# Attention steps of block 3 moved between slots, its last stores split between two queues, and its turned chunks placed elsewhere

## The chip, the core and the metric

The kernel runs on one core of one Trainium2 chip. Times are device microseconds of one launch; the profile is one execution taken by the hardware profiler, and its times count from the span's start. The engines are TensorE (PE, and PEld for its weight loads), VectorE (DVE), ScalarE (ACT), GpSimd (POOL) and SyncE (SP). SP computes nothing and issues DMAs; GpSimd and ScalarE issue DMAs too.

## What is computed

A normalized input goes through an attention over eight positions (two apart, looking back) and through a feed-forward layer with a squared ReLU. Both results and the input are added.

```python
def _A_ref(x, wqkv, wo):                 # S = 2048, D = 576, H = 32 heads of 18
    qkv = (x @ wqkv).reshape(B, S, 3, H, Dh)...
    idx = pos[:, None] - arange(8) * 2   # masked where negative
    logits = einsum("bhsd,bhswd->bhsw", q, kg) * Dh ** -0.5
    o = einsum("bhsw,bhswd->bhsd", softmax(logits), vg)
    return o.reshape(B, S, D) @ wo

def _B_ref(x, w1, b1, w2, b2):           # F = 4608
    r = max(x @ w1 + b1, 0)
    return (r * r) @ w2 + b2

xn = layernorm(x)
return x + _A_ref(xn, wqkv, wo) + _B_ref(xn, w1, b1, w2, b2)
```

## The kernel before

**Tiles and stages.** The sequence is cut into four blocks of 512 rows (b = 0 to 3), and the heads into four groups (g = 0 to 3). Matmuls have float32 accuracy from two parts: ScalarE copies a value to a rounded high part, VectorE subtracts that from the value and so makes the low part ("split", `..._hi` and `..._lo`); products are hi x hi, hi x lo and lo x hi. The feed-forward products of two blocks are combined so that fewer matmuls are needed (names T1 to T4, B11 to B22, `S`, `X`). The stages in order: the qkv products of blocks 0 and 1; `phase_a(0)`, feed-forward of both and second product of block 0; `phase_b0`, second product of block 1, then the qkv products of blocks 2 and 3 in four quarters ("quads"); `phase_a(1)`; `phase_b1`, which begins with `phase_blocks` (35 steps, k = 0 to 34, second product of blocks 2 and 3 in combined form) and ends block 3 with 16 "single tiles" (m = 0 to 15) of 14 matmuls each, the products with `wo` in five chunks c = 0 to 4, and `tail`.

**Attention on VectorE.** `attention(b, g)` is a generator of 19 steps: four times a product with the keys (`pr<-q,kv`) and its sum (`lg<-pr`), the maximum, the exponential on ScalarE, the division, then four times a product with the values (`pr<-lg,kv`) and three additions (`pr<-pr` twice, `q<-pr`). After the last additions the result q goes to DRAM in eight stores (`o<-q`), four for each of two parts of the columns. `side(n)` runs n steps where the code calls it, and tables of digits say how many: `QUADS` in the quads, `SPOTS` in `phase_a(1)`, `LAST` at the 35 steps k, `SINGLES` at the 16 tiles m. `complete(b)` runs what is left of a block's attention. The engines run their queues in the order in which the code is written.

**The end of block 3.** At m = `DUE`, or when no attention is left, `regroup(3, 0)` and `regroup(3, 1)` read the two stored parts back (`st<-o`, `r<-o`, issued by GpSimd). `o_hi(b, c)` turns a chunk with a transpose on VectorE (L1040, the last one L1045 with L1055 and L1056) and copies its high part on ScalarE; `o_lo` makes the low part on VectorE. `w2_hi` and `w2_lo` split the weights of the tile two ahead (w2s, three buffers: a split waits until TensorE has left the tile before the current one); `w2_lo` also issues the load of the tile five ahead (w2r, on SP). `h_hi` and `h_lo` split the next pair's operand (h). Chunk 4's weights are split last, at c = 2. In `tail` TensorE multiplies chunks 3 and 4, and drains and stores of the output follow.

Of the kernel before, what the change touches and what calls it, by code (L numbers as in the profile page):

```python
# [20 lines left out]
NB = S // TB  # L21
# [4 lines left out]
G = 4  # L26
# [6 lines left out]
L = P // G  # L33
# [11 lines left out]
ROWS = {(4 * b - 1 + k // 3, k % 3): (b, h) for b in (2, 3) for k, h in ((0, 0), (2, 2), (3, 1), (5, 2), (6, 2))}  # L45
PIECES = (0, 0, 0, 2, 3, 4, 0, 3, 2, 0, 2, 2, 1, 0, 3, 2, 4, 5)
SPOTS = ('000002', '120012', '100024', '010023', '110023', '111022', '110023', '100024', '010024', '120022', '110023', '110023', '120014', '110021', '110024', '110023', '110110', '000100')
QUADS = ('01111111111010', '10100010101110', '00110111111111', '10010000111111', '00000000000001', '00111010101010')
LAST = '00000111010011010011000101000011021'
SINGLES = '2222121212010000'  # L50
DUE = 10
TIMES = (2, 2, 3, 5, 6, 8, 10, 11, 14, 15, 17, 18, 19, 19, 22, 24, 27, 27, 29)
DRAINS = (14, 21, 24, 29, 26)
PAIRED = (*range(1, NP - 2, 2), NP - 2, NP - 1)
# [9 lines left out]
def block_kernel(ctx: ExitStack, tc: tile.TileContext, x, xt, wqkv, wo, w1, b1, w2, b2, w1l, w2q, w2l, w2x, out):  # L64
    nc = tc.nc
# [65 lines left out]
    def tt(out, a, b, op):  # L131
        return nc.vector.tensor_tensor(out=out, in0=a, in1=b, op=op)  # L132
# [18 lines left out]
    def four(dt=F32):  # L151
        return sb.tile([P, 2, TB], dt, name="r4", bufs=4)
# [210 lines left out]
    def shifted(t, j, *dims):  # L363
        a = t[:, j:j + 1, 0:1]
        return bass.AP(tensor=a.tensor, offset=a.offset, ap=[a.ap[0], [DIL * CG, W], *dims])

    loads, landed, queue, free, lane, kept_back = [], {}, [], [0], [nc.sync], [0]
# [17 lines left out]
    def release():  # L385
        free[0] += 1
        fetch()
# [10 lines left out]
    def attention(b, g):  # L398
        k, q = landed.pop(("k", b, g)), landed.pop(("q", b, g))
        lg = sb.tile([P, NA, W], F32, name="lg")  # L400
        mx = sb.tile([P, NA], F32, name="mx")
        sm = sb.tile([P, NA], F32, name="sm")
        for j in range(NJ):
            pr = sb.tile([P, W, CG], F32, name="pr")
            tt(pr, q[:, j:j + 1].to_broadcast([P, W, CG]), shifted(k, j, [1, CG]), ALU.mult)
            if j == NJ - 1:
                release()
            yield
            nc.vector.tensor_reduce(out=lg[:, j * HG:(j + 1) * HG].rearrange("p a w -> p w a"),  # L409
                                    in_=pr.rearrange("p w (a d) -> p w a d", d=DH), axis=AX.X, op=ALU.add)  # L410
            yield
        if b == 0:
            l4 = lg[:4].rearrange("p (j h) w -> p j h w", j=NJ)
            tt(l4, l4, mask[:4, :, None].to_broadcast([4, NJ, HG, W]), ALU.add)
        nc.vector.tensor_reduce(out=mx, in_=lg, axis=AX.X, op=ALU.max)
        tt(lg, lg, mx[:, :, None].to_broadcast([P, NA, W]), ALU.subtract)
        yield "exp"
        nc.scalar.activation(lg, lg, AF.Exp, scale=SCALE)
        yield
        nc.vector.tensor_reduce(out=sm, in_=lg, axis=AX.X, op=ALU.add)  # L420
        nc.vector.reciprocal(sm, sm)
        tt(lg, lg, sm[:, :, None].to_broadcast([P, NA, W]), ALU.mult)
        yield
        v = landed.pop(("v", b, g))
        for j in range(NJ):
            pr = sb.tile([P, W, CG], F32, name="pr")
            at = lg[:, j * HG:(j + 1) * HG].rearrange("p a w -> p w a")
            tt(pr.rearrange("p w (a d) -> p w a d", d=DH), at[:, :, :, None].to_broadcast([P, W, HG, DH]),
               shifted(v, j, [DH, HG], [1, DH]), ALU.mult)
            yield  # L430
            tt(pr[:, :4], pr[:, :4], pr[:, 4:], ALU.add)
            tt(pr[:, :2], pr[:, :2], pr[:, 2:4], ALU.add)
            tt(q[:, j], pr[:, 0], pr[:, 1], ALU.add)
            if j == NJ - 1:
                for k, (a, z) in enumerate(OPART):
                    rows = oscr[b, k][g * L:(g + 1) * L].rearrange("l (j i) c -> l i j c", i=G)
                    for i in range(G):
                        nc.gpsimd.dma_start(rows[:, i], q[i * L:(i + 1) * L, :, a:z])  # L438
                release()
            yield  # L440

# [3 lines left out]
    def side(k, exp=True):  # L445

        while k > 0:
            if current[0] is None:
                if not queue or queue[0][0] not in landed:
                    return k  # L450
                name, make = queue.pop(0)
                current[:] = [make(), None, name]
                steps_done[0] = 0
            if current[1] == "exp" and not exp:
                return k
            try:
                current[1] = next(current[0])
                steps_done[0] += 1
                k -= 1
            except StopIteration:  # L460
                current[0] = None
        return 0
# [564 lines left out]
    def o_hi(b, c):  # L1027
        if c == NC - 1 and b == 1:
            ot[b, c // 2] = sb.tile([P, 1, 1, TB], F32R, name="xf")
        elif c % 2 == 0:  # L1030
            ot[b, c // 2] = mt.tile([P, 2, 2, TB], F32R, name="h" if b == 1 else "w1s", bufs=3)
        hi = ot[b, c // 2][:, c % 2, 0]
        if c < NC - 1:
            if b != 1:
                of[b, c] = four()[:, 0]
            elif c % 2 == 0:
                t = four()
                of[b, c], of[b, c + 1] = t[:, 0], t[:, 1]
            src = ob[b, 0][:, :, c * L:(c + 1) * L] if c < 3 else ob[b, 1][:, :, :L]
            nc.vector.transpose(of[b, c].rearrange("p (u f) -> p u f", f=L), src)  # L1040
            nc.scalar.activation(hi, of[b, c], AF.Copy)
            return
        t = of[b, c] = four()
        n = L // 2
        nc.vector.transpose(t[:, 0].rearrange("p (u k f) -> p u k f", k=2, f=n),  # L1045
                            ob[b, 1][:, :, None, OB - n:].to_broadcast([P, NJ * G, 2, n]))
        nc.scalar.activation(t[:, 1].bitcast(F32R), t[:, 0], AF.Copy)

    def o_lo(b, c):
        hi = ot[b, c // 2][:, c % 2, 0]  # L1050
        t = of.pop((b, c))
        if c < NC - 1:
            tt(ot[b, c // 2][:, c % 2, 1], t, hi.bitcast(F32), ALU.subtract)
            return
        nc.vector.tensor_scalar(out=t[:, 0], in0=t[:, 0], scalar1=flip[:, 0:1], scalar2=None, op0=ALU.mult)  # L1055
        nc.vector.scalar_tensor_tensor(out=hi, in0=t[:, 1], scalar=flip[:, 1:2], in1=t[:, 0],  # L1056
                                       op0=ALU.mult, op1=ALU.add)
# [56 lines left out]
    def h_lo(s, p):  # L1114
        if p < NP:
            t = hs[s, p]
            tt(t[:, 1], t[:, 1].bitcast(F32), t[:, 0].bitcast(F32), ALU.subtract)
# [142 lines left out]
    def phase_b0():  # L1260
# [115 lines left out]
        def quads(k, half, some):  # L1376
            for n in some:
                s, i = steps[n]
                quad_step(k, s, 2 * half + i, i)
                side(int(QUADS[2 * k + half][n]))  # L1380
                hook(k, half, s, i)
# [183 lines left out]
    def phase_blocks():  # L1565
# [29 lines left out]
        for k in range(len(ORDER)):  # L1595
# [63 lines left out]
            if k == 32:  # L1659
                load_h(1, SINGLE[1])  # L1660
                h_hi(1, SINGLE[0])
                h_lo(1, SINGLE[0])
            side(int(LAST[k]))
        load_h(1, SINGLE[2])
# [3 lines left out]
    def phase_b1():  # L1668
        b = 3
        phase_blocks()  # L1670
        m = 0
        for j, p in enumerate(SINGLE):
            for f in range(2):
                w2_hi()
                if f == 0:
                    h_hi(1, SINGLE[j + 1] if j + 1 < len(SINGLE) else NP)
                add(b, tile_products(b, 2 * p + f, hs[1, p]))
                w2_lo()
                if f == 0:
                    h_lo(1, SINGLE[j + 1] if j + 1 < len(SINGLE) else NP)  # L1680
                elif j + 3 < len(SINGLE):
                    load_h(1, SINGLE[j + 3])
                if len(xr[b]) < 2 and (m == DUE or not queue and current[0] is None):
                    complete(b)
                    regroup(b, 0)
                    regroup(b, 1)
                    open_left(b)
                    load_left(b)
                for c in {13: (0,), 14: (1,), 15: (2,)}.get(m, ()):
                    o_hi(b, c)  # L1690
                    o_lo(b, c)
                side(int(SINGLES[m]))
                m += 1
        for c in range(NC - 2):
            w2_hi()
            add(b, o_ops(b, c), (NC - 2,) if c == NC - 3 else ())
            w2_lo()
            if c < 2:
                o_hi(b, c + 3)
                o_lo(b, c + 3)  # L1700
        tail()

    def tail():
# [211 lines left out]
    def q0():  # L1915
# [143 lines left out]
        def quads(half, which):  # L2059
            for n in which:  # L2060
                s, i = steps[n]
                quad_step(1, s, 2 * half + i, i, 0)
                side(int(QUADS[4 + half][n]))
                hook(half, s, i)
# [100 lines left out]
```

## Time and profile before

| | us |
|---|---|
| median of 3 timed runs | 1088.92 (1088.66 to 1090.38) |
| profiled execution, its own time | 1091.82 |
| its span | 1090.1 |
| busy: TensorE, VectorE, ScalarE, GpSimd | 1080.4, 941.7, 573.7, 156.5 |
| mean granted TensorE clock | 0.998 |
| chain that ended last | PE 88%, DVE 5%, DMA 3% |

TensorE is busy for 99% of the span, so the matmuls are nearly the whole time. The page's chain names VectorE and DMA for some 8%; where these stand, and what TensorE waits for, has to be read from the timelines. A busy engine off that chain, like VectorE with 86%, still decides when the next operand is there.

### The profile page before, as it was taken

The page shows a single profiled execution, that of the slowest core. Times are in us where ns is not written, and L with a number is a line of the kernel's source. Part 1 is how long each engine was busy: PE and PEld are TensorE (multiplying, and loading weights), DVE is VectorE, ACT ScalarE, POOL GpSimd, SP SyncE. Part 2 cuts the span into 40 slices and gives each one's busy share as a digit, 9 for nine tenths or more (in the row PEclk, how much of TensorE's full clock was granted, in tenths as well). Part 3 has the DMA queues.
Part 4 walks back from the last instruction along what each step waited for, and adds up shares of the span by engine and source line. Part 5 has one row for each costly group of instructions (what it writes and reads, how often), then busy time and mean ns, then how long its engine had stood idle before and what let it go on. Part 6 is the DMA issues. An engine that isn't in the chain of part 4 may idle for free.

```text
span 1090.1 us, 13936 instructions
## 1 busy us (share of the span) xinstructions
PE 1080.4 (99%) x4858; PEld 906.9 (83%) x4858; DVE 941.7 (86%) x1266; ACT 573.7 (53%) x808; POOL 156.5 (14%) x287
## 2 busy tenths in 40 slices
PE   9999999999999999999999999999999999999997
PEld 7998888888888888888899988888888788888886
DVE  7976899999999979999899688879888868999975
ACT  5555755656666564455345355555555565554332
POOL 5011220213130100002210302021022110000110
PEclk9999999999999999999999999999999999999999
DMA  8768998898898797867875889998998989776663
GB/s 282 259 202 298 328 358 297 318 354 289 288 367 320 273 357 236 282 218 261 307 221 166 327 301 399 365 345 323 367 360 307 361 299 360 274 219 205 221 191 102
DMA packets 107990, 316.33 MB, mean 290 GB/s; under 512 B 12880, under 2 KB 39504, under 8 KB 96016
## 3 DMA queue, kind: packets, MB, share of 16 engines
q1 hardware_dynamic: 72096, 205.96, 53.3%
q0 software_dynamic: 14640, 68.55, 17.3%
q10 hardware_dynamic: 21184, 40.94, 10.7%
q8 instruction: 38, 0.62, 0.2%
q14 instruction: 32, 0.26, 0.1%
HBM read 217.80 MB, written 97.60 MB: 289 GB/s over the span
## 4 chain that ended last, share of the span: by engine, by line
PE 88%; DVE 5%; DMA 3%; issue 2%; ACT 1%; POOL 0%; DVEq 0%; ACTq 0%; POOLq 0%
PE p L700 35%; PE p L591 28%; PE p L1575 9%; PE p L1216 9%; PE p L1911 2%; PE p L1220 2%; DMA w1s<-w 1%; DVE pr L132 1%; PE p L1821 1%; PE p L1966 1%; PE p L706 1%; DVE w2s L132 1%; DVE h L132 1%; DMA w2r<-in_wo 1%; DMA st<-o 0%
## 5 line engine op out<-in xcount | busy, mean ns | idle before, releaser
L591 PE MATMUL p<-h,w2s 128*128 128x512 f32 x1512 | 364.1, 389 | 0.0
L591 PEld LDWEIGHTS p<-h,w2s 128*128 128x128 f32 x1512 | 283.6, 188 | 60.0 <-ACT h L751 0.5
L700 PE MATMUL p<-X,w1s 128*128 128x512 f32 x864 | 219.7, 389 | 0.8 <-DMA w1s<-w 0.8
L700 PEld LDWEIGHTS p<-X,w1s 128*128 128x128 f32 x864 | 162.0, 188 | 35.4 <-ACT r L747 1.2
L700 PE MATMUL p<-S,w1s 128*128 128x512 f32 x648 | 166.0, 391 | 0.0
L700 PEld LDWEIGHTS p<-S,w1s 128*128 128x128 f32 x648 | 120.2, 188 | 28.4 <-ACT r L811 2.9
L563 ACT ACTIVATE w2s<-w2r 128x640 fp32r<-128x640 f32 x124 | 90.9, 734 | 82.2 <-PE p L591 63.7
L438 POOL DMA_DIRECT2D o<-q x128 | 69.6, 616 | 397.3 <-DVE q L132 396.4
L747 ACT ACTIVATE r<-r,b1t 128x512 f32<-128x512 f32 x72 | 52.2, 724 | 112.4 <-DVE r L132 112.2
L132 DVE TENSOR_TENSOR w2s<-w2r,w2s 128x576 fp32r<-128x576 f32 (+1 forms) x125 | 93.7, 751 | 13.9 <-ACT w2s L563 13.9
L132 DVE TENSOR_TENSOR h<-h 128x1024 fp32r<-128x1024 f32 (+1 forms) x84 | 80.3, 967 | 19.1 <-ACT h L764 13.0
L132 DVE TENSOR_TENSOR pr<-lg,kv 128x1152 f32<-128x1152 f32 x64 | 86.7, 1355 | 1.2
L132 DVE TENSOR_TENSOR pr<-q,kv 128x1152 f32<-128x1152 f32 x64 | 86.7, 1355 | 1.1
L409 DVE TENSOR_REDUCE lg<-pr 128x64 f32<-128x1152 f32 x64 | 86.4, 1350 | 1.0
L132 DVE TENSOR_TENSOR pr<-pr 128x576 f32<-128x576 f32 (+1 forms) x128 | 77.6, 606 | 3.2
L132 DVE TENSOR_TENSOR r<-p,r 128x512 f32<-128x512 f32 (+2 forms) x81 | 54.9, 681 | 19.6 <-ACT r L836 7.8
L755 ACT ACTIVATE r<-r 128x1024 f32<-128x1024 f32 x52 | 54.9, 1057 | 0.9
L811 ACT ACTIVATE r<-p 128x512 f32<-128x512 f32 x36 | 21.6, 599 | 57.2 <-PE p L700 57.2
L132 DVE TENSOR_TENSOR w1s<-w1r,w1s 128x1024 fp32r<-128x1024 f32 (+2 forms) x42 | 46.2, 1102 | 4.8 <-ACT w1s L527 4.3
L747 ACT ACTIVATE r<-p,b1t 128x512 f32<-128x512 f32 x72 | 48.3, 672 | 0.3 <-DMA out<-r 0.3
L836 ACT ACTIVATE r<-p 128x512 f32<-128x512 f32 x36 | 21.6, 600 | 49.8 <-PE p L700 49.8
L591 PE MATMUL p<-w1s,w2s 128*128 128x512 f32 x190 | 45.8, 400 | 1.9 <-DVE w2s L132 1.9
(280 smaller groups left out, 1546.9 us busy)
## 6 DMA issues: line engine op xcount, KB each, us to landing
kv<-kvq POOLq DMA_DIRECT2D x32, 1296.0 KB, 8.7
w2r<-in_w SPq DMA_DIRECT2D x104, 320.0 KB, 4.4
w<-w1s SPq DMA_DIRECT2D x21, 1024.0 KB, 6.9
w1s<-w ACTq DMA_DIRECT2D x19, 1024.0 KB, 8.5
h<-r SPq DMA_DIRECT2D x26, 512.0 KB, 6.7
h<-h SPq DMA_DIRECT2D x26, 512.0 KB, 4.4
w<-w1s SPq DMA_DIRECT2D x15, 768.0 KB, 8.2
w1s<-w ACTq DMA_DIRECT2D x15, 768.0 KB, 8.3
```

Source lines behind the costliest of these rows:

```text
L132: return nc.vector.tensor_tensor(out=out, in0=a, in1=b, op=op)
L409: nc.vector.tensor_reduce(out=lg[:, j * HG:(j + 1) * HG].rearrange("p a w -> p w a"), in_=pr.rearrange("p w (a d) -> p w a d", d=DH), axis ...
L438: nc.gpsimd.dma_start(rows[:, i], q[i * L:(i + 1) * L, :, a:z])
L563: nc.scalar.activation(w2s[stream[i]][:, :DE], raw2[i], AF.Copy)
L591: nc.tensor.matmul(yp[b][c], v, a, start=c not in yb[b], stop=c in last and c not in [o[0] for o in ops[i + 1:]], skip_group_check=True)
L700: nc.tensor.matmul(to, l, r, start=start and i == 0, stop=i == len(mm) - 1, skip_group_check=True)
L747: nc.scalar.activation(to, a, AF.Relu, bias=b1t[:, f:f + 1])
L755: nc.scalar.activation(r, r, AF.Square)
L1216: nc.tensor.matmul(to, l[:, js], r, start=start and n == 0, stop=n == len(mm) - 1, skip_group_check=True)
L1220: nc.tensor.matmul(to, v[:, js], ws[LEFT, f][:, n], start=False, stop=n == 1, skip_group_check=True)
L1575: nc.tensor.matmul(p, l, r, start=id(p) not in begun, stop=stop, skip_group_check=True)
L1911: nc.tensor.matmul(p[:, :QW], l, r, start=k == 0, stop=k == len(mm) - 1)
```

## The change

Four tables, a queue and the place of the turned chunks change. `QUADS` gives up one step in its third row, `LAST` takes one more at k = 28, `SINGLES` runs two steps in each of the first eight tiles and one in the ninth, and `DUE` is 9. The stores of the second part (k = 1) of block 3's last group go out on SP instead of GpSimd. Chunk 0 is turned at m = 14 instead of 13, chunk 1 at 15 instead of 14, chunks 2 and 3 both after chunk product 0, chunk 4 after product 1 as before.

```diff
-QUADS = (..., '00110111111111', ...)
-LAST = '00000111010011010011000101000011021'
-SINGLES = '2222121212010000'
-DUE = 10
+QUADS = (..., '00110111110111', ...)
+LAST = '00000111010011010011000101001011021'
+SINGLES = '2222222210000000'
+DUE = 9
...
-                        nc.gpsimd.dma_start(rows[:, i], q[i * L:(i + 1) * L, :, a:z])
+                        queue = nc.sync if k and (b, g) == (NB - 1, G - 1) else nc.gpsimd
+                        queue.dma_start(rows[:, i], q[i * L:(i + 1) * L, :, a:z])
...
-                for c in {13: (0,), 14: (1,), 15: (2,)}.get(m, ()):
+                for c in {14: (0,), 15: (1,)}.get(m, ()):
                     o_hi(b, c)
                     o_lo(b, c)
...
-            if c < 2:
-                o_hi(b, c + 3)
-                o_lo(b, c + 3)
+            for e in ((2, 3), (4,), ())[c]:
+                o_hi(b, e)
+                o_lo(b, e)
```

VectorE in the block products around k = 28 before: the low halves of two operands (h, then w1s) with a difference of weights (w2s) between them.

```order
L132 TENSOR_TENSOR w1r<-X_7705,w1r 128x1024
L132 TENSOR_TENSOR h<-h 128x1024
L132 TENSOR_TENSOR w2s<-w2s 128x512
L132 TENSOR_TENSOR w1s<-w1s 128x1024
L132 TENSOR_TENSOR mb<-w2s,mb 128x512
```

The same place in the changed kernel, on VectorE; pr and q are attention's.

```order
L132 TENSOR_TENSOR w1r<-X_7704,w1r 128x1024
L132 TENSOR_TENSOR h<-h 128x1024
L132 TENSOR_TENSOR pr<-pr 128x576
L132 TENSOR_TENSOR pr<-pr 128x288
L132 TENSOR_TENSOR q<-pr 128x144
L132 TENSOR_TENSOR w2s<-w2s 128x512
L132 TENSOR_TENSOR w1s<-w1s 128x1024
L132 TENSOR_TENSOR mb<-w2s,mb 128x512
```

The three additions of one attention step now stand between the two low halves.

VectorE at the end of attention before, from the last product with the values to the second turned chunk (w2s and h are the single tiles' splits, L1040 turns a chunk, w1s its low part).

```order
L132 TENSOR_TENSOR pr<-lg,kv 128x1152
L132 TENSOR_TENSOR w2s<-w2r,w2s 128x576
L132 TENSOR_TENSOR h<-h 128x1024
L132 TENSOR_TENSOR pr<-pr 128x576
L132 TENSOR_TENSOR pr<-pr 128x288
L132 TENSOR_TENSOR q<-pr 128x144
L132 TENSOR_TENSOR w2s<-w2r,w2s 128x576 x2
L132 TENSOR_TENSOR h<-h 128x1024
L132 TENSOR_TENSOR w2s<-w2r,w2s 128x576
L1040 STREAM_TRANSPOSE r_8987<-st 128x512
L132 TENSOR_TENSOR w1s<-r_8987,w1s 128x512
L132 TENSOR_TENSOR w2s<-w2r,w2s 128x576
```

The same stretch of VectorE in the changed kernel.

```order
L132 TENSOR_TENSOR pr<-lg,kv 128x1152
L132 TENSOR_TENSOR w2s<-w2r,w2s 128x576
L132 TENSOR_TENSOR pr<-pr 128x576
L132 TENSOR_TENSOR pr<-pr 128x288
L132 TENSOR_TENSOR q<-pr 128x144
L132 TENSOR_TENSOR w2s<-w2r,w2s 128x576
L132 TENSOR_TENSOR h<-h 128x1024
L132 TENSOR_TENSOR w2s<-w2r,w2s 128x576 x2
L132 TENSOR_TENSOR h<-h 128x1024
L132 TENSOR_TENSOR w2s<-w2r,w2s 128x576 x2
L1041 STREAM_TRANSPOSE r_9006<-st 128x512
L132 TENSOR_TENSOR w1s<-r_9006,w1s 128x512
```

One w2s and one h split have moved from ahead of the last q to behind it, and one more w2s split stands ahead of the first turned chunk.

SP's queue at the same time before (w2r are weight loads, h operand loads, x a piece of the input).

```order
L552 DMA w2r<-in_w 128x640 x2
L1107 DMA h<-h_194 128x1024
L552 DMA w2r<-in_w 128x640
L1082 DMA x_8925<-in_xt 64x512
L552 DMA w2r<-in_wo 128x640 x5
```

SP's queue there in the changed kernel.

```order
L553 DMA w2r<-in_w 128x640 x2
L1108 DMA h<-h_194 128x1024
L439 DMA o_107<-q 128x1x48 x4
L1083 DMA x_8904<-in_xt 64x512
L553 DMA w2r<-in_w 128x640
L553 DMA w2r<-in_wo 128x640 x5
```

The four stores came in ahead of x, and the last load of a single tile's weights moved behind both.

## Rows read from the trace of the kernel before

**Rows 1.** Waits of PE, whole span: us in total, times, longest us.

```profile
PE p L591 <- DVE w2s L132: 1.9, 1, 1.9
```

**Rows 2.** Timeline of PE at the end: start us, us, what, count, [idle before].

```profile
1016.83 50.96 PE L591 MATMUL p<-h,w2s 128*128 128x512 f32 x224
1067.62 10.13 PE L591 MATMUL p<-w1s,w2s 128*128 128x512 f32 x44
1079.65 5.52 PE L591 MATMUL p<-w1s,w2s 128*128 128x512 f32 x16 [1.90 <-DVE w2s L132]
1085.01 1.35 PE L1720 MATMUL p<-w1s,w2s 128*128 128x256 f32 x10
```

**Rows 3.** Windows: us, busy by engine, granted clock (PEclk), DMA share, GB/s.

```profile
1080.80:1081.50 0.70, 0.70 (x3) 0.57 (x2) 0.67 (x2) 0.00 (x0) 0.00 (x0) 0.50 0.00 0
...
847.00:848.50 1.50, 0.74 (x3) 0.67 (x4) 1.16 (x3) 1.47 (x2) 0.00 (x0) 1.00 0.97 406
```

**Rows 4.** Timeline of DVE, end of attention and turned chunks.

```profile
1049.44 1.36 DVE L132 TENSOR_TENSOR pr<-lg,kv 128x1152 f32<-128x1152 f32 x1
1050.71 0.75 DVE L132 TENSOR_TENSOR w2s<-w2r,w2s 128x576 fp32r<-128x576 f32 x1
1051.38 1.22 DVE L132 TENSOR_TENSOR h<-h 128x1024 fp32r<-128x1024 f32 x1
1052.52 1.24 DVE L132 TENSOR_TENSOR pr<-pr 128x576 f32<-128x576 f32 x2
1053.80 0.31 DVE L132 TENSOR_TENSOR q<-pr 128x144 f32<-128x144 f32 x1
...
1065.36 0.71 DVE L1040 STREAM_TRANSPOSE r<-st 128x512 f32<-128x512 f32 x1 [5.53 <-DMA st<-o]
...
1078.85 0.75 DVE L132 TENSOR_TENSOR w2s<-w2r,w2s 128x576 fp32r<-128x576 f32 x1
```

**Rows 5.** Timeline of POOL, last stores and read-back.

```profile
1054.40 4.34 POOL L438 DMA_DIRECT2D o<-q  x8 [33.39 <-DVE q L132]
1059.99 0.56 POOL L1023 DMA_DIRECT2D st<-o  x1 [1.26 <-DMA o<-q]
```

**Rows 6.** Chain that ended last, in order of time: start us, us, what.

```profile
1055.96 3.49 DMA o<-q
...
1059.99 5.34 DMA st<-o
```

**Rows 7.** Timeline of DVE, block products around k = 28.

```profile
991.55 0.29 DVE L132 TENSOR_TENSOR xf<-w2s,xf 128x128 fp32r<-128x128 f32 x1 [1.26 <-ACT xf L136]
...
997.44 1.22 DVE L132 TENSOR_TENSOR h<-h 128x1024 fp32r<-128x1024 f32 x1
...
999.18 1.22 DVE L132 TENSOR_TENSOR w1s<-w1s 128x1024 fp32r<-128x1024 f32 x1
...
1007.11 1.25 DVE L132 TENSOR_TENSOR pr<-pr 128x576 f32<-128x576 f32 x2
...
1008.62 1.22 DVE L132 TENSOR_TENSOR h<-h 128x1024 fp32r<-128x1024 f32 x1
1011.33 1.23 DVE L132 TENSOR_TENSOR h<-h 128x1024 fp32r<-128x1024 f32 x1 [1.50 <-ACT h L1112]
```

**Rows 8.** Timeline of PE, start of step k = 31.

```profile
1002.27 1.52 PE L1575 MATMUL p<-w1s,w1r 128*128 128x512 f32 x6
```

**Rows 9.** Timeline of SP, load of the first single tiles' operand.

```profile
1004.59 0.45 SPq L1107 DMA_DIRECT2D h<-h  x1
```

**Rows 10.** Timeline of ACT, what waits for that load.

```profile
1010.24 1.06 ACT L1112 ACTIVATE h<-h 128x1024 fp32r<-128x1024 f32 x1 [6.21 <-DMA h<-h]
```

**Rows 11.** The page's DMA issues: count, KB each, median us to landing.

```profile
kv<-kvq POOLq DMA_DIRECT2D x32, 1296.0 KB, 8.7
w2r<-in_w SPq DMA_DIRECT2D x104, 320.0 KB, 4.4
```

**Rows 12.** Instructions on o, 1015.5 to 1020.3 us: eight stores before.

```profile
DMA to landing us min/median/max: 1.9/3.4/4.2
```

More of the change, by code (lines that the diff above doesn't have):

```diff
@@ L47 @@
 SPOTS = ('000002', '120012', '100024', '010023', '110023', '111022', '110023', '100024', '010024', '120022', '110023', '110023', '120014', '110021', '110024', '110023', '110110', '000100')
-QUADS = ('01111111111010', '10100010101110', '00110111111111', '10010000111111', '00000000000001', '00111010101010')
-LAST = '00000111010011010011000101000011021'
-SINGLES = '2222121212010000'
-DUE = 10
+QUADS = ('01111111111010', '10100010101110', '00110111110111', '10010000111111', '00000000000001', '00111010101010')
+LAST = '00000111010011010011000101001011021'
+SINGLES = '2222222210000000'
+DUE = 9
 TIMES = (2, 2, 3, 5, 6, 8, 10, 11, 14, 15, 17, 18, 19, 19, 22, 24, 27, 27, 29)
```

## Prediction

> **What bounds the kernel now.** I read TensorE's waits over the whole span first. It hardly ever waits; the largest wait but the one at the start is 1.9 us for VectorE's half of a weight tile w2s [rows 1]. So only the place of that wait can give much. TensorE's timeline shows it: 224 matmuls of the 16 single tiles run from 1016.83, 44 of the output chunks from 1067.62, then nothing until 1079.65, then 16 and 10 more [rows 2]. The pace is 50.79 us / 224 = 0.227 us for a matmul, but the 16 behind the wait take 1085.01 - 1079.65 = 5.36 us, not 16 x 0.227 = 3.63 us. The windows tell why: shortly behind the wait the granted clock is 0.50 (1.2 GHz); around a gap in the middle, in which TensorE was busy for 0.74 of 1.50 us, it stayed at 1.00 (2.4 GHz) [rows 3]. So the wait cost 1.90 us and the low clock behind it 5.36 - 3.63 = 1.73 us, 3.63 us together.
>
> What the wait hangs on shows on VectorE, on GpSimd and in the chain. Attention of block 3 ends on VectorE with the last q at 1053.80 + 0.31 = 1054.11 [rows 4]. GpSimd issues eight stores from 1054.40; the fourth, at 1055.96, lands 3.49 us later; the read-back st<-o is issued at 1059.99 and takes 5.34 us [rows 5, 6], to 1065.33. VectorE, idle for 5.53 us, turns the first chunk at 1065.36 and ends the last weight split at 1078.85 + 0.75 = 1079.60 [rows 4]: 14.24 us in which VectorE and ScalarE take turns. TensorE wants that split at about 1067.62 + 10.13 = 1077.75 [rows 2].
>
> **The change, part by part.**
>
> *One attention step is taken out in the third quarter of the qkv products and given back at k = 28 of the block products.* Between the two places the same steps run one slot later. In a queue that runs in order, the attention work ahead of any other VectorE instruction is then one step less, never more, so TensorE, which almost never waits there, loses nothing: cost 0. A gain is excluded for the same reason; a loss needs an attention step that itself meets a wait, and I keep 0.3 us for it in the range.
>
> *The step given back.* At k = 28 VectorE is not ahead in spite of the smaller load: it stood idle for 1.26 us before 991.55, held by ScalarE and no shortage of its own, and that brings both versions to the same time. So the step, three additions, lies between the split h at 997.44 and the rest, at 1008.62 - 1007.11 = 1.51 us. The next split that TensorE needs is w1s at 999.18, ended 1000.40 [rows 7], now 1001.9. TensorE starts on that operand at 1002.27 [rows 8] and takes its low half second, near 1002.5: some 0.6 us to spare, cost 0, but thin. Behind it all of VectorE's work is 1.51 us later, and so are SP's loads, which wait for VectorE's splits in turn, h<-h at 1004.59 among them [rows 9]; ScalarE waited 6.21 us for it [rows 10], and VectorE 1.50 us for ScalarE before 1011.33 [rows 7]. That idle time moves along and swallows nothing, so I carry the whole 1.51 us into the single tiles. If the load were not behind it, up to 1.5 us would come back: bounds 0 and 1.51.
>
> *SINGLES and DUE.* Attention takes two steps in each of the first eight single tiles and one in the ninth, so the split w2s at 1050.71 and the split h at 1051.38 fall behind the last q: 1052.52 - 1050.71 = 1.81 us less [rows 4]. The last q then ends at 1054.11 + 1.51 - 1.81 = 1053.8. Splits of the tiles before come later. The closest is tile 10: back from 1053.8 stand the three additions (1.59), a split (0.67), a product (1050.71 - 1049.44 = 1.27) and the split h (1.14), so that its weights are split by 1049.1. TensorE reaches tile 10 at 1016.83 + 10 x 3.174 = 1048.6 and the low half four matmuls later, 1049.5: cost 0 with 0.4 us to spare.
>
> *Stores on two queues.* GpSimd issues four stores, SP the four of the other part. The read-back waits for the landing of the first part alone: GpSimd stood idle for 1.26 us before it, until a landing, not for issues of its own [rows 5]. So the split as such takes nothing off the chain; it brings forward the second read-back, wanted only for the fourth chunk. On SP the four stand ahead of x, of one w2r load for a single tile and of the five for the chunks. That load goes out near 1056, lands 4.4 us later [rows 11] at 1060.4, and two splits of 0.75 us later tile 15 has it, which is due at 1016.83 + 15 x 3.174 = 1064.4: cost 0 with 2.5 us of cover.
>
> The Trainium skill, DMA: Bandwidth & Descriptors, section "Issuing engines are not separate DMA queues", says that transfers run on the same 16 engines whoever issues them, and that several issuers save issue time only. The idle 1.26 us agrees. A reader who credited the split with half of GpSimd's 4.34 us would land the read-back 2.2 us earlier than I do below; the rule speaks against that.
>
> The landing of the fourth store is the uncertain term. The stores of the attention before, among loads, took 1.9 to 4.2 us [rows 12]; here it was 3.49 with loads in between. Now a w2r and an h load go out just ahead of the stores, three w2r loads after them. I take 2.7, midway between 1.9 and 3.49. The first issue is 0.29 us after q, the fourth 1.56 later: 1053.8 + 0.29 + 1.56 + 2.7 = 1058.35. The read-back goes out 0.54 later, 1058.9, and with 5.34 us as before is there at 1064.2, against 1065.33. With 1.9 us it is 1063.4, with 4.2 us 1065.7.
>
> *The turned chunks.* The split of the first chunk's weights now comes before the first turn, in idle time, and the third and fourth chunk stand back to back. That takes one split, 1051.38 - 1050.71 = 0.67 us, out of the 14.24: 13.57. The fifth chunk's weights are ready at 1064.2 + 13.57 = 1077.8, against a demand at 1077.75. Much earlier is no use: the split of the third chunk's weights cannot start before TensorE has left the last single tile at 1067.62, a floor near 1077.4. With the read-back at 1065.7 they are ready at 1079.3, a wait of 1.5 us.
>
> **Sum against the profiled execution** (1091.82 us: 1090.1 span, 1.72 around it). The wait shrinks from 1.90 to about 0.1, so -1.8; a wait that short is below the gap that left the clock alone, so -1.73: 1088.3. The median of the timed runs, 1088.92, lies 2.9 us below the profiled one, and these runs spread from 1088.66 to 1090.38, 1.72 us, as much as the low clock costs. So some of them may have kept the clock. If the median's run lost it, the new time is 1088.92 - 3.5 = 1085.4; if not, 1088.92 - 1.8 = 1087.1. I can't tell the two apart, give them the same weight, and forecast the value between them, 1086.3.
>
> **Rivals.**
> 1. *The landing is hardly earlier* (1065 to 1065.7). For it: the push of 1.51 us eats most of the 1.81, and six loads share the stretch with the stores. Against it: loads that lay between the stores now follow them. The wait is then 0.85 to 1.5 us and the clock falls as often as now: 0.4 to 1.05 us gained, 1087.9 to 1088.5.
> 2. *Slower: the read-back meets the loads.* Three w2r loads and the second read-back are in flight with it, closer than before. If it takes what the 1296 KB reads take, 8.7 us [rows 11], it is there at 1058.9 + 8.7 = 1067.6, the weights are ready at 1081.2 and the wait is 3.4 us: 1088.92 + 1.5, and 1.7 more if the median had kept the clock; 1090.4 to 1092.1. Against it: 5.34 us was measured with two such loads in flight. It decides from a read-back of 7.1 us on, where the wait is as long as now.
> 3. *A new wait at k = 31 or in the single tiles.* The push is larger than the 0.4 to 0.6 us to spare. A late split costs its lateness once, say 0.5 us, and the end gains as forecast: 1086.8.
> 4. *Attention ends no tile sooner.* The program's order has the two splits behind the last q, so only the times can undo it, and that is rival 1.
>
> **How the numbers follow.** Forecast 0.56 (half near 1085.4, half near 1087.1); rival 1 0.25; rival 2 0.11; rival 3 0.08. A difference of 0.2%, 2.2 us, is about what a measurement of this kernel can tell from none: faster is below 1086.7, slower above 1091.1. Faster: half of the forecast, a third of its other half, half of rival 3 and a tenth of rival 1: 0.28 + 0.09 + 0.04 + 0.02 = 0.43. Slower: half of rival 2, 0.06. Same: 0.51. The range goes from the floor with the clock kept, 1088.92 - 3.63 less 0.5 for the spread of runs, 1084.8, to the worst of rival 1 and the 0.3 us of the first part, 1088.8; it leaves out rival 2 and the tails.
>
> **What would show it.** Right: the last q near 1053.8; the read-back there near 1064; a wait before the fifth chunk under 0.5 us and the clock at 1.00 to the end; TensorE done near 1082.7 in place of 1086.4. The push shows as the step at k = 28 ending near 1000.1 and the split h at 1012.8 in place of 1011.33. Wrong: a wait of over 0.8 us still there (rival 1), a read-back of 7 us or more (rival 2), waits of TensorE between 1002 and 1060 (rival 3), or a last q at 1052.3, which would say that the push was swallowed.

## The result, and the profile after

| | before | changed |
|---|---|---|
| median of 13 runs, us | 1089.15 (1087.51 to 1091.55) | 1091.45 (1090.51 to 1094.70) |
| profiled execution, its own time | 1091.82 | 1091.57 |

The ratio is 1.0022, with a 95% interval of 1.0012 to 1.0031: the change makes the kernel 0.2% slower, 2.3 us in the medians. I had forecast 1086.3 and a range of 1084.8 to 1088.8.

The two profiled executions must not be subtracted: the one of before was a bad draw of its kernel. It lost 1.73 us to the low clock [rows 3]; of the 117 runs of before that stood beside the experiments, 103 have a mean granted clock of 0.999 or 1.000, and the 14 with 0.998 all took 1089.9 us or more. So the traces are compared stretch by stretch. I set the start of each of the 4858 matmuls of the changed kernel against the same matmul before. Up to 765 us the difference stays within 0.35 us; then the changed kernel falls back by 0.34 us between 765 and 780, by 0.20 between 815 and 840, by 0.98 between 840 and 868 and by 0.21 near 1000, and the single tiles begin at 1018.26 instead of 1016.83 [rows 2].

The 0.98 us understate the loss, because the execution of before waits in the same stretch for a load:

```profile
847.76 1.62 PE L700 MATMUL p<-X,w1s 128*128 128x512 f32 x6 [0.84 <-DMA w1s<-w]
```

Only two of the other 15 traces have such a wait there, of some 0.4 us. Against the version called base below, whose trace has none, the changed kernel loses 2.1 us between 840 and 868.

TensorE's waits in the changed kernel (us in total, times, longest) show a new one beside the one that is answered by [rows 1]:

```profile
PE p L701 <- ACT p L789: 1.5, 1, 1.5
PE p L592 <- DVE w2s L132: 1.5, 1, 1.5
```

The new wait is for ScalarE. First TensorE's, then ScalarE's timeline there (start us, us, what, [idle before <- what ended it]):

```profile
852.57 1.65 PE L701 MATMUL p<-S,w1s 128*128 128x512 f32 x6 [1.54 <-ACT p L789]
```

```profile
849.17 1.06 ACT L752 ACTIVATE h<-r 128x1024 fp32r<-128x1024 f32 x1 [2.17 <-DMA op<-h]
850.27 1.06 ACT L756 ACTIVATE r<-r 128x1024 f32<-128x1024 f32 x1
851.23 0.67 ACT L748 ACTIVATE r<-p,b1t 128x512 f32<-128x512 f32 x1
851.93 0.58 ACT L789 ACTIVATE p<-p 128x512 f32<-128x512 f32 x1
```

ScalarE writes the high part of h (`square_hi`, L752) only once a DMA has landed, a store of h to scratch memory (`op<-h`). The copy p<-p that TensorE needs stands three instructions behind it. In the kernel before the same instruction waits for nothing of the kind:

```profile
846.09 0.72 ACT L747 ACTIVATE r<-r,b1t 128x512 f32<-128x512 f32 x1 [2.54 <-DVE r L132]
846.85 1.06 ACT L751 ACTIVATE h<-r 128x1024 fp32r<-128x1024 f32 x1
```

The page's chain of the changed kernel names that store, and the read-back, by itself (start us, us, what):

```profile
837.47 11.62 DMA op<-h
...
1059.37 7.65 DMA st<-o
```

The end of TensorE's timeline answers [rows 2], and one window [rows 3]:

```profile
1018.26 50.96 PE L592 MATMUL p<-h,w2s 128*128 128x512 f32 x224
1069.06 10.13 PE L592 MATMUL p<-w1s,w2s 128*128 128x512 f32 x44
1080.67 3.94 PE L592 MATMUL p<-w1s,w2s 128*128 128x512 f32 x16 [1.48 <-DVE w2s L132]
1084.45 1.35 PE L1721 MATMUL p<-w1s,w2s 128*128 128x256 f32 x10
```

```profile
1080.80:1081.50 0.70, 0.70 (x4) 0.56 (x5) 0.70 (x2) 0.00 (x0) 0.00 (x0) 1.00 0.00 0
```

The wait is still 1.48 us, and the clock stayed at 1.00 behind it. VectorE [rows 4], GpSimd [rows 5] and SP show what it hangs on:

```profile
1054.45 0.31 DVE L132 TENSOR_TENSOR q<-pr 128x144 f32<-128x144 f32 x1
...
1067.05 0.71 DVE L1041 STREAM_TRANSPOSE r<-st 128x512 f32<-128x512 f32 x1 [2.44 <-DMA st<-o]
...
1079.86 0.75 DVE L132 TENSOR_TENSOR w2s<-w2r,w2s 128x576 fp32r<-128x576 f32 x1
```

```profile
1055.05 2.17 POOL L439 DMA_DIRECT2D o<-q  x4 [31.51 <-DVE q L132]
1059.37 0.56 POOL L1024 DMA_DIRECT2D st<-o  x1 [2.15 <-DMA o<-q]
```

```profile
1054.79 2.59 SPq L439 DMA_DIRECT2D o<-q  x4
1057.42 0.60 SPq L1083 DMA_DIRECT2D x<-in_xt  x1
1058.13 0.53 SPq L553 DMA_DIRECT2D w2r<-in_w  x1
1058.76 4.54 SPq L553 DMA_DIRECT2D w2r<-in_wo  x3
```

Counted from the start of the single tiles, the last q is done 36.50 us later (before 37.28), the read-back is there 48.76 us later (before 48.50). Attention ends sooner, and the gain is gone before the data is back: the read-back took 7.65 us instead of 5.34 [rows 6].

### The profile page after: what moved, and what is told of

It reads as the page before. It is cut to its first block, busy times and chain, and to the rows that moved or that the text cites. A ratio compares the mean times of both kernels' runs of the same rounds, so it can differ in the third digit from the quotient of the medians.

```text
span 1089.8 us, 13938 instructions
## 1 busy us (share of the span) xinstructions
PE 1079.2 (99%) x4858; PEld 905.7 (83%) x4858; DVE 942.0 (86%) x1266; ACT 574.3 (53%) x808; POOL 154.5 (14%) x283
## 4 chain that ended last, share of the span: by engine, by line
PE 81%; DVE 8%; DMA 6%; issue 3%; ACT 1%; POOL 0%; ACTq 0%; SPq 0%; DVEq 0%; POOLq 0%
PE p L701 32%; PE p L592 25%; PE p L1217 9%; PE p L1576 7%; DVE pr L132 2%; PE p L1912 2%; PE p L1221 2%; DVE h L132 1%; DVE w2s L132 1%; DMA w1s<-w 1%; DMA op<-h 1%; PE p L1967 1%; PE p L707 1%; DMA st<-in_w2l 1%; DVE lg L409 1%
## 5 line engine op out<-in xcount | busy, mean ns | idle before, releaser
L439 POOL DMA_DIRECT2D o<-q x124 | 67.4, 614 | 386.8 <-DVE q L132 385.9
L132 DVE TENSOR_TENSOR r<-p,r 128x512 f32<-128x512 f32 (+2 forms) x81 | 54.9, 681 | 24.2 <-ACT r L837 11.9
L378 POOL DMA_DIRECT2D kv<-kvq x32 | 19.0, 599 | 193.8 <-DVE pr L132 155.4
```

What stands on the lines that cost most here:

```text
L439: queue.dma_start(rows[:, i], q[i * L:(i + 1) * L, :, a:z])
```

## Experiments

All are compared with runs of the kernel before on the same chip. The versions ran in four sets on four chips (e1 to e4, e5 to e8, e9 to e12, e13 and e14); across sets the ratios compare better than the medians, since the median of the kernel before itself goes from 1089.15 to 1089.81. "Base" is the kernel before with the new SINGLES, DUE and chunk order alone.

**Parts of the change, alone and left out.** `e1_no_lag` is the changed kernel with the old QUADS and LAST; `e2_lag_only` is the kernel before with the new ones:

```diff
-QUADS = (..., '00110111111111', ...)
-LAST = '00000111010011010011000101000011021'
+QUADS = (..., '00110111110111', ...)
+LAST = '00000111010011010011000101001011021'
```

> The changed kernel with QUADS and LAST as before: no step is taken out in the third quarter and none given back at k = 28. Theory A (the lag costs): with it the stores of an attention group go out a slot later, the 1296 KB load behind them on GpSimd 1.7 us later, and it meets the weight loads and the stores of h around 835 to 850 us, so that ScalarE waits for a store and TensorE 1.54 us for ScalarE at 852.57. Without the lag this wait is gone, the single tiles start near 1016.8 instead of 1018.26, and the time is 1.2 to 1.5 us below the changed kernel, near 1090.0, the read-back still taking over 7 us because of SP's stores. Rival (the wait at 852 is an accident of one execution; the loss is at the end): the time stays within 0.5 us of the changed kernel's 1091.45.

> The kernel before with the new QUADS and LAST alone. Theory A: TensorE waits about 1.5 us near 852 for ScalarE's copy, the single tiles start 1.2 to 1.5 us later than 1016.83, the last q is later by 1.2 to 3 us (the step at k = 28 comes on top), the wait at the end stays near 1.9 or grows, and the time is 1.2 to 2.5 us above the kernel before: 1090.4 to 1091.7. Rival: no difference to the kernel before within 0.5 us.

Measured: 1087.96 us without the lag, ratio 0.9987 (0.9978 to 0.9996), and 1094.22 with the lag alone, ratio 1.0038 (1.0026 to 1.0051), against 1089.81. The lag (the step taken out early and given back late) costs 3.5 to 4.4 us in these medians, more than I expected of it. The 4.4 hold a part for the clock: all six runs of e2 have a mean clock of 0.998, but only four of the 26 of before. e1's read-back took 8.3 us. In e2 the wait of 1.5 us for ScalarE is there, behind another wait of ScalarE for `op<-h`:

```profile
852.20 1.06 ACT L751 ACTIVATE h<-r 128x1024 fp32r<-128x1024 f32 x1 [2.18 <-DMA op<-h]
```

`e3_no_queue` leaves all stores on GpSimd; `e4_singles_chunks` is the base:

```diff
-                        queue = nc.sync if k and (b, g) == (NB - 1, G - 1) else nc.gpsimd
+                        queue = nc.gpsimd
```

> The changed kernel with all eight last stores on GpSimd again. Theory B (the queue costs): SP's four stores hold back its weight loads, which then go out bunched together with the read-back and stretch it from 5.34 to 7.65 us. With the stores on GpSimd the read-back takes 5.3 to 6 us and is there near 1065.2 to 1066, the wait before the fifth chunk falls from 1.48 to under 0.4 us, and the time is 1.1 to 1.5 us below the changed kernel, near 1090.1. Rival (the read-back is late for another reason, as its fourth store lands late): read-back 7 us or more, time within 0.5 us of the changed kernel's.

> The kernel before with SINGLES, DUE and the chunk order of the change alone: no lag, no second queue. If A and B both hold, the single tiles start near 1016.8, the last q stands near 1052.3, the read-back is there near 1063, the wait at the end is under 0.3 us, and the time is 1.5 to 1.9 us below the kernel before, 1087.2 to 1087.7, more if the kernel before has lost the clock in its median run. If only one of A and B holds, it lies 1.2 to 1.5 us higher, at 1088.6 to 1089.1. If neither holds, it is as slow as the changed kernel, 1091.4.

Measured: 1090.76 (ratio 1.0004, 0.9995 to 1.0013), half the gain that I expected over the changed kernel, and 1087.09 (ratio 0.9979, 0.9970 to 0.9989). Without SP's stores the read-back took 4.5 and 5.9 us, and the wait before the fifth chunk is gone in both. The base is 2.7 us faster than the kernel before in the medians; these are all the waits of TensorE over 0.15 us that its trace has:

```profile
PE p L1739 <- DVE lg L1732: 2.1, 1, 2.1
PE p L1576 <- DVE h L132: 0.3, 1, 0.3
```

**What in the lag costs.** The expectations above blame the later stores and loads of attention for the wait at 852. The order in which the program hands out buffers offered another reason. Tile h has three buffers; in the second feed-forward stage (pairs p of tiles) three kinds of tile take them in turn, at lines of the changed kernel: the high part of r squared (call it h0, L752), which TensorE reads, a tile t (L887), which the store at L769 reads, and y (L765), which a second store reads. Before, h0 of a pair always stands where the last h0 stood, and waits for TensorE. With the lag h0 stands at p = 8 and at p = 14 where t stood, and waits for t's store; in the trace the store has landed in time at p = 8, but not at p = 14. ScalarE's order at p = 14, before and changed, with what each instruction waits for (DMAHW is a DMA's completion, r and p are temporaries):

```
L751 ACTIVATE h<-r_7312 128x1024 [waits PE_49,Activation_49]

L752 ACTIVATE h<-r_7310 128x1024 [waits DMAHW2_49,Activation_49]
```

Three runs have a part of the lag, with the buffers as before. All start from the base; one digit of SPOTS (steps in the second feed-forward stage) gives back or takes out a step:

```diff
 e5: QUADS as changed; SPOTS[3]
-'010023'
+'110023'
 e6: SPOTS[6], SPOTS[15]
-'110023', '110023'
+'100023', '210023'
 e7: LAST as changed; SPOTS[15]
-'110023'
+'010023'
```

> The kernel before with the new SINGLES, DUE and chunk order (as in the run without lag and without a second queue, 1087.1 us), and the lag over the quads alone: the step is taken out in the third quarter and given back at p = 3 of the second feed-forward stage, not at k = 28. Theory R (the buffers): a lag that is still open at p = 8 and p = 14 makes the program hand ScalarE's high part of h the buffer that the store of an earlier product has just left, so that ScalarE waits for the store's landing and TensorE 1.3 to 1.5 us for ScalarE near 852. Here the buffers rotate as before, so no such wait, and 1087.1 to 1087.6. Theory D (the later stores and kv loads of attention overload the DMA engines in every stretch with a lag): part of the 3.7 us that the lag costs shows already, 1088.3 or more.

> The same base, with one attention step taken out at p = 6 of the second feed-forward stage and given back at p = 15: around 800 to 855 us attention stands exactly as in the changed kernel, a step late, stores and kv loads too, but the buffers of h rotate as before. Theory R: ScalarE does not wait for a store of h near 849, TensorE does not wait for ScalarE near 852, and the time is 1087.1 to 1087.9. Theory D: the kv load goes out 1.7 us later, meets the weight loads and stores, and TensorE waits 1 us or more in sum between 800 and 860; 1088.5 to 1090.8.

> The same base, with one attention step taken out at p = 15 and given back at k = 28, so the step at k = 28 comes without the lag ahead. My prediction's term (b): VectorE is 1.51 us later behind k = 28, the last q as much later, and TensorE loses nothing but some 0.1 to 0.3 us at k = 30, where the three lagging versions waited 0.38 to 0.40 us against 0.23 to 0.34 without; since the wait at the end was below nothing by some us of reserve, the time is 1087.1 to 1087.6. Rival: the push uses up the reserve at the end and the wait comes back, 1088 to 1090.

Measured: 1087.62 (ratio 0.9984, 0.9974 to 0.9994), 1088.25 (0.9985, 0.9977 to 0.9994) and 1087.99 (0.9982, 0.9970 to 0.9994), against 1089.31. No trace has a wait for ScalarE near 852, e6's neither, though attention stands there as in the changed kernel, and none has the wait before the fifth chunk. By their times alone the theories are not told apart: e6's 1088.25 lies between the two spans that I gave, e7's 1087.99 above mine. The medians are 0.5 to 1.2 us above the base's 1087.09, which the ratios do not tell apart.

The decisive pair has the lag from p = 6 to k = 28 and differs in one step at p = 3, which stands at the fifth place in e9 and at the sixth in e10. That suffices to turn the buffers:

```diff
 both: base, QUADS and LAST as changed, SPOTS[6] '100023'; SPOTS[3]
-'010033'
+'010024'
```

> The kernel before with the new SINGLES, DUE and chunk order and with nearly the whole lag: the step is taken out in the third quarter, given back at p = 3 (its fifth place) and taken out again at p = 6, and given back for good at k = 28. From p = 6 to k = 28 attention stands as in the changed kernel. The buffers of h rotate as in the kernel before: ScalarE's high part of h at p = 14 waits for TensorE, not for a store. Theory R (the buffers): no wait of TensorE for ScalarE near 852, and 1087.6 to 1088.6, like the three runs with a part of the lag. Rival D (the lag itself, whatever the buffers): as slow as the whole lag without a second queue, 1090.3 to 1091.3.

> The same as the run lag_old_buffers, but the step at p = 3 is given back one place later, at the sixth instead of the fifth. That alone makes the program hand out the buffers of h as in the changed kernel: at p = 8 and p = 14 ScalarE's high part of h gets the buffer that a store has just read. Theory R: ScalarE waits about 2 us for that store near 849, TensorE 1.2 to 1.6 us for ScalarE near 852, and the time is 1.3 to 3 us above that of lag_old_buffers. Rival D: the two take the same time within 0.5 us.

Measured: 1087.48 (ratio 0.9987, 0.9979 to 0.9996) and 1090.91 (1.0015, 1.0006 to 1.0024), against 1089.48: 3.4 us apart, a little more than the 1.3 to 3 that I gave. ScalarE's copy into h, e9 and then e10:

```profile
846.82 1.06 ACT L752 ACTIVATE h<-r 128x1024 fp32r<-128x1024 f32 x1
```

```profile
849.96 1.06 ACT L752 ACTIVATE h<-r 128x1024 fp32r<-128x1024 f32 x1 [2.40 <-DMA op<-h]
```

The stores of h took nearly as long in both, 11.1 to 11.4 us and 11.9 to 12.0 us, so it is not mainly their landing that makes the difference but who has to wait for it. In e10's profiled execution the clock fell behind the wait as well. TensorE and the windows around it:

```profile
853.35 2.52 PE L701 MATMUL p<-S,w1s 128*128 128x512 f32 x6 [1.54 <-ACT p L789]
```

```profile
850.00:853.00 3.00, 1.55 (x6) 0.66 (x4) 1.22 (x2) 2.94 (x4) 0.00 (x0) 1.00 1.06 428
853.50:854.50 1.00, 1.00 (x4) 0.78 (x5) 0.00 (x0) 1.00 (x3) 0.00 (x0) 0.67 1.00 423
```

Six matmuls took 2.52 us instead of 1.6. The low clock does not make the difference of the medians: eight of e10's eleven runs have a mean clock of 1.000 and a median of 1090.78, e9's nine such runs 1087.91. Nor does another stretch: of the 4.5 us between the two traces 3.9 lie between 840 and 868 us (1.7 of them the low clock). So most of the loss does not come from the lag as such, but from the buffers that it turns. (Another tile, r with four buffers, is handed out differently too; no wait in the traces names it. Which of the free buffers a tile gets is settled when the program is built; I take it that it goes by the order in which they come free, and have not tested that.)

**Singles and chunks apart.** `e8_singles_only` has the new SINGLES and DUE, `e12_chunks_only` the new chunk order, each on the kernel before.

```diff
 e8
-SINGLES = '2222121212010000'
-DUE = 10
+SINGLES = '2222222210000000'
+DUE = 9
 e12
-                for c in {13: (0,), 14: (1,), 15: (2,)}.get(m, ()):
+                for c in {14: (0,), 15: (1,)}.get(m, ()):
...
-            if c < 2:
-                o_hi(b, c + 3)
-                o_lo(b, c + 3)
+            for e in ((2, 3), (4,), ())[c]:
+                o_hi(b, e)
+                o_lo(b, e)
```

> The kernel before with the new SINGLES and DUE alone, chunks in the old order. By my terms (c) and (e): attention ends 1.8 us sooner, the read-back too, and the chain behind it takes 14.24 us instead of 13.57, so the split of the fifth chunk's weights ends about 1.1 us before TensorE wants it in place of 1.9 us too late; the time is that of both together, 1087.1 to 1087.5. Rival (the chunk order carries the gain): a wait of 0.5 to 1.5 us stays at the end, 1087.6 to 1088.7.

> The kernel before with the new chunk order alone. By my term (e): the chain from the first turned chunk to the last weight split takes 13.57 us instead of 14.24, the wait at the end shrinks by 0.6 to 0.7 us, and the time is 0.6 to 1.0 us below the kernel before, 1088.3 to 1088.8, less often with a low clock. Rival (the order does nothing without the earlier end of attention): within 0.3 us of the kernel before.

Measured: 1087.99 (ratio 0.9990, 0.9979 to 1.0001) with a wait of 0.6 us left at the end, and 1088.66 (0.9996, 0.9987 to 1.0004) with 1.22 us. Neither differs from the kernel before with certainty; the base, which has both, does, and has no wait there. I had expected no wait in e8; its read-back took 6.3 us instead of 5.34, and its time lies in the rival's span. e12 came as expected. Its row at the end of TensorE:

```profile
1077.78 3.96 PE L591 MATMUL p<-w1s,w2s 128*128 128x512 f32 x16 [1.22 <-DVE w2s L132]
```

**The queue.** `e11_act_queue` is e1 with `nc.scalar` in place of `nc.sync`. `e14_late_stores` is e1 with SP's four stores and the second read-back two tiles later:

```diff
-                    regroup(b, 1)
                     open_left(b)
                     load_left(b)
+                if m == DUE + 2:
+                    for rows, part in late:
+                        nc.sync.dma_start(rows, part)
+                    regroup(b, 1)
```

> The run without lag, but with the four last stores of the second part issued by ScalarE instead of SP. Theory B (order on SP): SP's four stores keep its weight loads back by 2.5 us, so that three of them go out within 1.5 us of the read-back, which then takes 7.65 to 8.28 us instead of 4.5 to 5.87. With the stores on ScalarE the loads go out as early as with all stores on GpSimd: the read-back takes 5 to 6.3 us, the wait at the end is gone, and the time is 1087.0 to 1087.6. Rival (two queues of stores as such, and the second read-back that follows closer, stretch it): 7 us or more, a wait of 0.5 us or more at the end, 1087.9 or more.

> The run without lag, but SP issues its four stores, and GpSimd the read-back of the second part, two tiles later: behind x and two weight loads instead of ahead of them. Theory B (SP's stores hold its loads back and bunch them into the read-back): the loads go out as early as with all stores on GpSimd, one at most within 1.5 us ahead of the read-back, which then takes 4.5 to 6.3 us, is there by 1061.5 when tile times are as in that run, and the wait at the end is below 0.3 us: 1086.9 to 1087.6. Rival (two stores queues or stores on SP stretch the read-back whatever stands behind them): 7 us or more and 1087.8 to 1088.3.

Measured: e11 took 1089.57 (ratio 1.0009, 0.9998 to 1.0020). Its read-back took 5.6 us, as expected, but the stores wait in ScalarE's queue for q, with the copies of the next weights and of h behind them:

```profile
1051.25 2.63 ACTq L439 DMA_DIRECT2D o<-q  x4
1053.98 0.74 ACT L564 ACTIVATE w2s<-w2r 128x640 fp32r<-128x640 f32 x1 [8.33 <-issue]
1054.63 1.04 ACT L1113 ACTIVATE h<-h 128x1024 fp32r<-128x1024 f32 x1
```

TensorE then waits 1.3 us for that h:

```profile
PE p L592 <- ACT h L1113: 1.3, 1, 1.3
```

So e11 shows a wait of its own making, and tells only that two store queues do not stretch the read-back. e14 took 1087.62 (0.9983, 0.9973 to 0.9993) and its read-back 5.9 us, with one load in the 1.5 us before it was issued at 1058.32, where the changed kernel has three (the rows of SP above). But the data was hardly sooner there: with the loads ahead of them the first part's stores now took 4.3 to 4.8 us, where they took 2.4 to 2.7 in e1, GpSimd stood idle for 4.2 us before the read-back, and a wait of 0.5 us stayed at the end, which neither theory had. Early loads slow the stores, late loads the read-back. In the base, with all stores on GpSimd, SP's loads go out like this, x ahead of the stores (from 1050.07), and one of them, at 1054.55, in the 1.5 us before the read-back at 1055.48:

```profile
1049.15 0.51 SPq L1083 DMA_DIRECT2D x<-in_xt  x1
1050.47 0.33 SPq L553 DMA_DIRECT2D w2r<-in_w  x1
1052.28 5.77 SPq L553 DMA_DIRECT2D w2r<-in_wo  x3
```

**All parts, old buffers.** `e13_all_old_buffers` is e9 with SP's stores, so it has every part of the change.

> The changed kernel with all its parts, but with two attention steps placed so that the buffers of h rotate as in the kernel before: one step is given back at p = 3 (fifth place) and taken out again at p = 6 of the second feed-forward stage. If the buffers are what turns the change from a gain into a loss, TensorE does not wait for ScalarE near 852 and the time is 2.8 to 3.5 us below the changed kernel's 1091.45: 1088.0 to 1088.7, of which 0.7 to 0.9 us are the price of the second queue, so the read-back takes over 7 us again and a wait of 0.3 to 1.2 us stands before the fifth chunk. If the change loses for another reason too, it stays above 1089.5. My prediction for the change was 1086.3.

Measured: 1089.13 (ratio 0.9998, 0.9989 to 1.0007, against 1089.39), 2.3 us below the changed kernel, but 0.4 above the span that I gave. The wait at 852 is gone, the one at the end is 0.8 us, and the read-back took 6.9 us. So the queue takes back most of what the rest gains: e9 without it is 1.65 us faster in the medians, 1.2 by the ratios.

## Why the prediction was wrong

- **The moved step: cost 0, at most 0.3. This is the step that failed.** I followed VectorE's queue alone ("in a queue that runs in order ... TensorE loses nothing"). A moved instruction also changes which buffer a tile gets, and so what another engine waits for: e10 against e9 gives 3.4 us for that in the medians (3.0 by the ratios). In the traces the stretch from 840 to 868 us takes 1.6 to 3.8 us longer in the four versions with the turned buffers than in the middle one of the nine others that have no wait there (1.6 to 2.1 with the clock kept). The rest of the 3.4 us is not placed. None of my rivals was this.
- **The same step, on VectorE's queue itself: wrong too, by little.** The lag costs 0.34 to 0.39 us between 765 and 780 us in all seven traces in which it is open there, and 0.03 at most in the eight others. What TensorE waits for shows on VectorE, which takes two products out of their banks p (`r<-p,r`); TensorE's next product into such a bank waits for that. Before:

```profile
758.84 0.69 DVE L132 TENSOR_TENSOR r<-p,r 128x512 f32<-128x512 f32 x1 [0.59 <-PE p L700]
768.89 0.69 DVE L132 TENSOR_TENSOR r<-p,r 128x512 f32<-128x512 f32 x1
770.79 1.52 PE L700 MATMUL p<-X,w1s 128*128 128x512 f32 x6
```

Changed:

```profile
758.55 0.69 DVE L132 TENSOR_TENSOR r<-p,r 128x512 f32<-128x512 f32 x1 [0.36 <-PE p L701]
769.97 0.68 DVE L132 TENSOR_TENSOR r<-p,r 128x512 f32<-128x512 f32 x1
770.71 1.65 PE L701 MATMUL p<-X,w1s 128*128 128x512 f32 x6
```

The two stand 10.05 us apart before and 11.42 in the changed kernel; TensorE had 1.2 us to spare before, and in the changed kernel it starts 0.06 us after the second is done. One step less is ahead of the first in the changed kernel, but that head start is gone there, since VectorE waits for TensorE all the same. Between the two stand as many steps as before, but before one of them is the exponential, which runs on ScalarE; in the changed kernel all of them are VectorE's, with one product of 1.35 us more. So "one step less, never more" is right as a count from the start, and wrong from one wait to the next.
- **The step at k = 28: right.** It ends at 1001.60 us, where I had 1000.1; some 1.2 us of that is the lateness that TensorE brought along. From the start of the single tiles the last q stands 36.54 us away in e7 against 35.09 in the base: 1.45 us pushed, where I had 1.51 [rows 7]. Nothing swallowed it, and TensorE's wait near 998 us is as long in e7 (0.29) as in the base (0.30).
- **SINGLES and DUE: right, a little more.** 35.09 us in the base and in e8 against 37.28 before, 2.19 us sooner, where I had 1.81.
- **The queue: cost nothing, read-back 5.34 as before. The second step that failed.** My estimate of 2.7 us for the fourth store was even too long, it landed in 2.2. But SP's stores, 2.59 us of issue that had to wait for q, held x and the weight loads back; in the changed kernel three of these went out in the last 1.3 us ahead of the read-back. It took 7.65, 8.3 and 6.9 us in the three versions with SP's stores in that place (the changed kernel, e1, e13), and 4.5 to 6.3 in the thirteen others. From the last q to the data in place it is 12.3, 13.0 and 11.7 us in the three, and 10.2 to 12.1 in the eleven with GpSimd alone. That is the mechanism of rival 2, whose chance I put at 0.11, with 7.1 us as the point of decision. That the measured 1091.45 lies in rival 2's span, 1090.4 to 1092.1, is luck: the queue costs 0.7 to 2.0 us in the pairs below, and the larger part of the loss comes from the buffers.
- **The rule that I weighed against the queue.** The Trainium skill (DMA: Bandwidth & Descriptors, "Issuing engines are not separate DMA queues") says that transfers share the same engines and interleave, whichever engine issued them, and that several issuers save issue time alone. I used its second half and stopped short of the first. In e1 the read-back goes out 4.75 us after the last q instead of the base's 5.70, but not by issue time: GpSimd issues its fourth store 1.86 us after q in e1 and 1.85 in the base, and it lands in 2.35 us instead of 3.31, with the loads behind it. Those loads then meet the read-back, and the data is there 13.0 us after q instead of 11.6.
- **The chunk order: right.** From the first turn to the end of the last split it takes 1079.86 + 0.75 - 1067.05 = 13.56 us in the changed kernel, as I had (13.57); e12's wait of 1.22 us is the old 1.90 less the 0.67 of one split.
- **The median: half wrong.** I left open whether it had lost the clock. By all that is on record it had not, since 1088.92 lies below each of the 14 runs of before with a mean clock of 0.998; so only the wait could be won, not the 1.73 us of the low clock. That my figure for this half, 1087.1, is what the base gives (1087.09) is luck in part: the base has neither the moved step nor the second queue, and the kernel before took 1089.81 beside it.

The terms add up, as far as the runs can tell. In the medians: base -2.7, lag with the old buffers +0.4 (e9 against the base), turned buffers +3.4, queue +0.7 (the changed kernel against e3; 0.9 and 1.65 in the other pairs), in all +1.8 to +2.8, against +2.3 measured. By the ratios, which take the differences between the sets out: -2.3, +0.9, +3.0, and +2.0, 0.9 and 1.2 for the queue, in all +2.5 to +3.6, against +2.4. Each ratio is uncertain by some 1 us, so the single terms are known no better than that. The best version is the base, 1087.09 us: 0.21% faster than the kernel before, and faster than the changed one.

## What to carry to other kernels

A moved instruction does not only wait and make wait on its own engine: where tiles rotate through buffers, set the other engines' orders with their waits side by side before and after, and look for a wait that now names a DMA instead of an engine. On the engine itself, compare the work between two of its waits and not the work since the start, for a head start ends at the next wait. Stores given to a queue that also issues loads delay those loads by the stores' own wait, and the loads then fall on the transfer that the stores were to speed up. And before crediting a change with a low clock's return, look at the clock of the timed runs, not at that of the profiled one.

## What the runs showed of the chip

TensorE's clock fell to 0.50 (1.2 GHz) behind the waits of 1.90 us [rows 1, 3] and 1.97 us (e2) at the end, and behind two that ended near 543 us, of 1.89 us in e5 and 2.40 us in e8; it stayed at 1.00 behind the 1.48 and 1.54 us of the changed kernel and the 1.54 us near 855 in e2. In e10 a wait of the same 1.54 us cost the clock, after TensorE had been busy for 1.55 of 3.00 us; the shorter neighbour wait of 0.25 us was the only difference to the changed kernel that I found. Between 837 and 850 us, where the DMA share is 0.94 to 1.01, the two stores of h take 9.5 to 14.4 us to land in the 16 traces, so a buffer that has to be stored first is out of use for that long.
